# Retention followed by token mixing on one core: decay folded into q and v, head pairs on 128 partitions, and a hand-ordered pipeline of the two stages

## The chip, the cores and the metric

The kernel runs on one core of a Trainium2 chip. The metric is the device time of one launch in microseconds; in every run on record it is 1.65 to 1.84 us longer than the span of the same execution, which goes from the first to the last instruction. PE is TensorE (matrix products and transposes), PEld its weight loads, DVE is VectorE, ACT is ScalarE, POOL is GpSimd, and SP issues the transfers. A run counts as slow when it is over 1.5% above the fastest of its kernel; all times and ratios compared below are of fast executions, unless a median is called that of all runs.

## The reference

Eight heads of retention run over 768 tokens for each of four batches. The output, with the heads side by side, is the input of a mixing layer.

```python
gamma = 1.0 - 2.0 ** (-5.0 - np.arange(H))                 # H = 8, S = 768, D = 64, B = 4
for t in range(S):                                         # retention
    state = gamma * state + k_t (outer) v_t
    y[t] = scale * q_t @ state
x = y with heads joined                                    # B x 768 x 512
theta = x @ w_theta                                        # 512 x 512
zr, zi = x * cos(theta), x * sin(theta)
u = x + w_tok_r @ zr + w_tok_i @ zi                        # 768 x 768, over the tokens
out = u + relu(u @ w_ch)                                   # 512 x 512
```

Retention is computed in chunks of 128 tokens: products inside a chunk with a decay mask, and a state that carries the earlier chunks. There are 24 chunks and 24 mixing tiles of 128 tokens. A mixing tile needs all six chunks of its batch.

## The kernel before

All weights are loaded and transposed first. Then each batch runs the whole of retention and after it the whole of mixing.

```python
        for b in range(B):
            for c in range(nT):                       # retention, six chunks
                # ... load k, v, q of the chunk; one cast on ACT into kvq
                for src, dst, sc in ((kkc, kT, None), (qtmp, qTsc, qscale)):
                    tps = attPS.tile([D, H, P], BF, name="tps", bufs=2)
                    for h in range(H):                # 16 transposes, 64 wide
                        nc.tensor.transpose(tps[:, h, :],
                                            src[:, h * D : (h + 1) * D], ident)
                    # ... copy (k) or product with the decay (q) on DVE
                # ... kks = k times the decay, on POOL
                at_ps = attPS.tile([P, H, P], FT, name="at_ps", bufs=1)
                for h in range(H):                    # 8 score products, 64 deep
                    nc.tensor.matmul(at_ps[:, h, :], kT[:, h, :], qTsc[:, h, :], ...)
                nc.vector.tensor_mul(at, at_ps, Ddiag)
                # ... 8 value products, 8 state reads, 4 transposes of x, 8 state updates
            for t0 in range(nT):                      # theta, six tiles
                th_ps = moePS.tile([P, dm], FT, name="th_ps", tag="at_ps")
                # ... 4 matmuls; cos and sin on ACT; two products on DVE
            for t0 in range(nT):                      # token mixing, six tiles
                # ... 12 matmuls; u = y + x on DVE; 4 transposes of u; copy
            for t0 in range(nT):                      # channel mixing, six tiles
                # ... 4 matmuls; relu on ACT; sum on DVE; store
```

Of the kernel before, what the change touches and what calls it, by code (L numbers as in the profile page):

```python
# [19 lines left out]
PI = math.pi  # L20


def _bf16_view(ap: bass.AP) -> bass.AP:
    t = dataclasses.replace(ap.tensor, shape=list(ap.tensor.shape))
    ap2 = bass.AP(tensor=t, offset=ap.offset, ap=[list(p) for p in ap.ap])
    ap2 = ap2.bitcast(BF)
    new_pat = [list(p) for p in ap2.ap]
    new_pat[-1][0] *= 2
    new_pat[-1][1] //= 2
    return bass.AP(tensor=ap2.tensor, offset=ap2.offset + 1, ap=new_pat)  # L30


def _bcast_free(ap: bass.AP, n: int) -> bass.AP:
    return bass.AP(tensor=ap.tensor, offset=ap.offset,
                   ap=list(ap.ap) + [[0, n]])
# [3 lines left out]
def kernel(  # L39
# [10 lines left out]
):  # L50
    nc = tc.nc
# [5 lines left out]
    HD = dm  # L57
    HDp = HD + D
    scale = 1.0 / math.sqrt(D)
    gammas = [1.0 - 2.0 ** (-5.0 - h) for h in range(H)]  # L60

    qb = _bf16_view(q)
    kb = _bf16_view(k)
    vb = _bf16_view(v)


    const = ctx.enter_context(tc.tile_pool(name="const", bufs=1))

    ident = const.tile([P, P], BF)
    make_identity(nc, ident)  # L70
    identf = const.tile([P, P], FT)
    make_identity(nc, identf)

    iota_pp = const.tile([P, P], FT)
    nc.gpsimd.iota(iota_pp, pattern=[[0, P]], base=0, channel_multiplier=1,
                   allow_small_or_imprecise_dtypes=True)
    iota_f = const.tile([P, P], FT)
    nc.gpsimd.iota(iota_f, pattern=[[1, P]], base=0, channel_multiplier=0,
                   allow_small_or_imprecise_dtypes=True)
    colS_iota = const.tile([P, nT], FT)  # L80
    nc.gpsimd.iota(colS_iota, pattern=[[-P, nT]], base=127, channel_multiplier=-1,
                   allow_small_or_imprecise_dtypes=True)
    halfpi = const.tile([P, 1], FT)
    nc.gpsimd.memset(halfpi, PI / 2.0)
    lscale = const.tile([P, 1], FT)
    nc.gpsimd.memset(lscale, math.log(scale))
    zerob = const.tile([P, 1], FT)
    nc.gpsimd.memset(zerob, 0.0)

    Ddiag = const.tile([P, H, P], FT)  # L90
    qscale = const.tile([P, H, P], BF)
    colS = const.tile([P, nT, H], FT)
    gshift = const.tile([D, nT, H], FT)
    for h in range(H):
        g = gammas[h]
        lg = math.log(g)
        nc.scalar.activation(Ddiag[:, h, :], iota_pp, AF.Exp, bias=zerob, scale=-lg)
        nc.gpsimd.tensor_scalar(Ddiag[:, h, :], Ddiag[:, h, :], scalar1=1.0 / g,
                                scalar2=None, op0=ALU.mult)
        nc.gpsimd.affine_select(  # L100
            out=Ddiag[:, h, :], in_=Ddiag[:, h, :],
            compare_op=ALU.is_ge, fill=0.0, base=0,
            pattern=[[1, P]], channel_multiplier=-1,
        )
        nc.scalar.activation(qscale[:, h, :], iota_f, AF.Exp, bias=lscale, scale=lg)
        nc.gpsimd.tensor_scalar(qscale[:, h, :], qscale[:, h, :], scalar1=g,
                                scalar2=None, op0=ALU.mult)
        nc.scalar.activation(colS[:, :, h], colS_iota, AF.Exp, bias=zerob, scale=lg)
        for c in range(nT):
            nc.gpsimd.memset(gshift[:, c, h : h + 1], g ** (P * c))  # L110

    wconst = ctx.enter_context(tc.tile_pool(name="wconst", bufs=1))
    wth = wconst.tile([P, nD, dm], BF)
    wch = wconst.tile([P, nD, dm], BF)
    wtr = wconst.tile([P, nT, S], BF)
    wti = wconst.tile([P, nT, S], BF)

    with (
        tc.tile_pool(name="attA", bufs=2) as attA,
        tc.tile_pool(name="attB", bufs=2) as attB,  # L120
        tc.tile_pool(name="attPS", bufs=1, space=bass.MemoryType.PSUM) as attPS,
    ):
        for d0 in range(nD):
            for src, dst in ((moe_w_theta, wth), (moe_w_ch, wch)):
                tmp = attA.tile([P, dm], FT, name="wtmp")
                nc.sync.dma_start(out=tmp, in_=src[d0 * P : (d0 + 1) * P, :])
                nc.vector.tensor_copy(dst[:, d0, :], tmp)
        for src, dst in ((moe_w_tok_r, wtr), (moe_w_tok_i, wti)):
            for t0 in range(nT):
                tmp = attA.tile([P, S], FT, name="wtmpw")  # L130
                nc.sync.dma_start(out=tmp, in_=src[t0 * P : (t0 + 1) * P, :])
                wkrow = attA.tile([P, S], BF, name="wkrow")
                nc.vector.tensor_copy(wkrow, tmp)  # L133
                tp = attPS.tile([P, nT, P], BF, name="wtps", tag="tps", bufs=2)
                for s0 in range(nT):
                    nc.tensor.transpose(tp[:, s0, :],  # L136
                                        wkrow[:, s0 * P : (s0 + 1) * P], ident)
                nc.vector.tensor_copy(dst[:, :, t0 * P : (t0 + 1) * P], tp)
        for b in range(B):
            state_bf = attB.tile([D, H, D], BF, name="state_bf")  # L140
            st_ps = attPS.tile([D, H, D], FT, name="st_ps", bufs=1)
            x_sb = attB.tile([P, nT, dm], BF, name="x_sb")
            xT = attB.tile([P, nD, S], BF, name="xT")

            for c in range(nT):
                kvqin = attA.tile([P, 3 * HD], FT, name="kvqin")
                nc.sync.dma_start(
                    out=kvqin[:, :HD].rearrange("p (h d) -> p h d", h=H),
                    in_=k[b, :, c * P : (c + 1) * P, :].rearrange("h s d -> s h d"))
                nc.sync.dma_start(  # L150
                    out=kvqin[:, HD : 2 * HD].rearrange("p (h d) -> p h d", h=H),
                    in_=v[b, :, c * P : (c + 1) * P, :].rearrange("h s d -> s h d"))
                nc.sync.dma_start(
                    out=kvqin[:, 2 * HD :].rearrange("p (h d) -> p h d", h=H),
                    in_=q[b, :, c * P : (c + 1) * P, :].rearrange("h s d -> s h d"))
                kvq = attA.tile([P, 3 * HD + D], BF, name="kvq")
                nc.scalar.copy(kvq[:, : 3 * HD], kvqin)  # L157
                kkc = kvq[:, :HDp]
                vvc = kvq[:, HD : HD + HDp]
                qtmp = kvq[:, 2 * HD : 2 * HD + HDp]  # L160
                kT = attA.tile([D, H, P], BF, name="kT")
                qTsc = attA.tile([D, H, P], BF, name="qTsc")
                for src, dst, sc in ((kkc, kT, None), (qtmp, qTsc, qscale)):
                    tps = attPS.tile([D, H, P], BF, name="tps", bufs=2)
                    for h in range(H):
                        nc.tensor.transpose(tps[:, h, :],  # L166
                                            src[:, h * D : (h + 1) * D], ident)
                    if sc is None:
                        nc.vector.tensor_copy(dst, tps)
                    else:  # L170
                        nc.vector.tensor_mul(dst, tps, sc[:D])  # L171
                kks = attA.tile([P, HDp], BF, name="kks")
                nc.gpsimd.tensor_mul(  # L173
                    kks[:, :HD].rearrange("p (h d) -> p h d", h=H),
                    kkc[:, :HD].rearrange("p (h d) -> p h d", h=H),
                    _bcast_free(colS[:, c], D))

                at_ps = attPS.tile([P, H, P], FT, name="at_ps", bufs=1)
                for h in range(H):
                    nc.tensor.matmul(at_ps[:, h, :], kT[:, h, :], qTsc[:, h, :],  # L180
                                     start=(h % 4 == 0), stop=(h % 4 == 3),
                                     skip_group_check=True)
                at = attA.tile([P, H, P], BF, name="at")
                nc.vector.tensor_mul(at, at_ps, Ddiag)  # L184

                y_ps = attPS.tile([P, H, D], FT, name="y_ps", bufs=2)
                last = (c == 0)
                for h in range(H):
                    nc.tensor.matmul(y_ps[:, h, :], at[:, h, :],  # L189
# [10 lines left out]
                for d0 in range(nD):  # L200
                    nc.tensor.transpose(tpf[:, d0, :],
                                        x_sb[:, c, d0 * P : (d0 + 1) * P], ident)
# [88 lines left out]
```

## Time and profile before

| | before |
|---|---|
| time, median of 3 runs | 314.29 us |
| span of the profiled execution | 318.5 us |
| mean granted PE clock | 0.885 |
| PE busy | 235.5 us (74%), 1832 matmuls |
| DVE, ACT, POOL busy | 174.9, 86.2, 42.0 us |
| share of the chain that is not PE | 45% |

The lines are shown in the prediction below. In a strip, each digit is the busy share of a fortieth of the span in tenths. The chain starts at the last instruction and goes back, at each step to what released it. In a row of a stretch, each engine has its busy microseconds and in brackets its number of instructions; the granted clock and the DMA share follow.

The profiled execution of the kernel before would itself count as slow: a span of 318.5 us makes a time of some 320 us, where the fastest run took 313.55 us. The views of the profiled execution are read here for what waits for what, not to the per cent.

### The profile page before, as it was taken

The numbers are of one execution on the slowest core, as the hardware profiler recorded it, in microseconds if no ns is written. First come the engines' busy times: TensorE is split into PE (matmuls) and PEld (weight loads), VectorE is DVE, ScalarE is ACT, GpSimd is POOL, SyncE is SP. The second block draws the span as 40 slices with busy tenths as digits, with TensorE's granted clock in tenths as the row PEclk, the third lists the DMA queues.
The fourth block names the chain that finished last, engine by engine and source line by source line (L and its number), as shares of the span: only waits on it lengthen the run. The fifth ranks groups of instructions, "written<-read, shape, count | busy, mean of one in ns | idle before, by whom it ended". The sixth has DMA issues, their size and how long they took to land.

```text
span 318.5 us, 4555 instructions
## 1 busy us (share of the span) xinstructions
PE 235.5 (74%) x1832; PEld 140.0 (44%) x1832; DVE 174.9 (55%) x292; ACT 86.2 (27%) x122; POOL 42.0 (13%) x110
## 2 busy tenths in 40 slices
PE   0344677975699589886898578658985997778981
PEld 0222566842244368642343467323434785223430
DVE  2754557763444588843344899534347887233342
ACT  8000421236301231344102333441022330331022
POOL 8830221111000021210000022200000220000000
PEclk9999999979999975659999998799999657558999
DMA  6889975774000457763002298640013620000013
GB/s 225 271 258 254 195 151 112 149 141 99 1 2 12 155 126 160 151 125 66 2 0 94 107 197 184 117 99 0 2 66 132 145 55 3 0 0 1 2 66 132
DMA packets 81238, 32.28 MB, mean 101 GB/s; under 512 B 75585, under 2 KB 75585, under 8 KB 81217
## 3 DMA queue, kind: packets, MB, share of 16 engines
q1 hardware_dynamic: 81216, 31.99, 41.0%
q8 instruction: 14, 0.23, 0.3%
q14 instruction: 8, 0.06, 0.1%
HBM read 25.69 MB, written 6.29 MB: 100 GB/s over the span
## 4 chain that ended last, share of the span: by engine, by line
PE 55%; DVE 19%; DMA 12%; ACT 9%; issue 3%; SPq 0%; POOL 0%; ACTq 0%; DVEq 0%
PE moe_y L238 10%; PE moe_y L241 10%; PE th_ps L223 9%; PE tps L166 7%; DMA out_dram<-ot 5%; DVE at L184 5%; PE at_ps L180 4%; DMA wtmpw<-in_moe_w_tok_r_dram 4%; ACT cos_t L228 4%; PE y_ps L189 4%; DVE ot L259 3%; ACT kvq L157 3%; PE y_ps L195 3%; DVE zr L230 2%; PE tpf L247 2%
## 5 line engine op out<-in xcount | busy, mean ns | idle before, releaser
L238 PE MATMUL moe_y<-zr,wtr 128*128 128x512 bf16 x144 | 46.5, 398 | 18.0 <-DVE zr L230 18.0
L157 ACT CAST kvq<-kvqin 128x1536 bf16<-128x1536 f32 x24 | 35.3, 1472 | 90.0 <-PE y_ps L189 62.4
L173 POOL TENSOR_TENSOR kks<-kvq,colS 128x512 bf16<-128x512 bf16 x24 | 25.0, 1042 | 218.5 <-ACT kvq L157 218.5
L166 PE MATMUL tps<-ident,kvq 128*64 128x128 bf16 x384 | 40.9, 274 | 8.2 <-ACT ot L258 5.5
L166 PEld LDWEIGHTS <-kvq 128*64 128x64 bf16 x384 | 32.9, 144 | 13.8 <-issue 8.9
L258 ACT ACTIVATE ot<-o_ps 128x512 f32<-128x512 f32 x24 | 14.3, 597 | 84.9 <-PE o_ps L254 66.6
L241 PE MATMUL moe_y<-zi,wti 128*128 128x512 bf16 x144 | 35.6, 379 | 0.0
L223 PE MATMUL th_ps<-wth,xT 128*128 128x512 bf16 x96 | 33.3, 482 | 1.3 <-ACT sin_t L229 1.3
L184 DVE TENSOR_TENSOR at<-at_ps,Ddiag 128x1024 bf16<-128x1024 f32 x24 | 29.2, 1218 | 5.7 <-PE at_ps L180 5.1
L244 DVE TENSOR_TENSOR u<-moe_y,x_sb 128x512 bf16<-128x512 f32 x24 | 16.6, 691 | 26.8 <-PE moe_y L241 26.8
L230 DVE TENSOR_TENSOR zr<-x_sb,cos_t 128x512 bf16<-128x512 bf16 x24 | 10.8, 449 | 36.9 <-ACT cos_t L228 36.9
L228 ACT ACTIVATE cos_t<-th_ps,halfpi 128x512 bf16<-128x512 f32 x24 | 16.5, 688 | 52.4 <-PE th_ps L223 52.4
L254 PE MATMUL o_ps<-wch,uT 128*128 128x512 bf16 x96 | 23.3, 378 | 5.8 <-ACT ot L258 5.6
L136 PE MATMUL wtps<-ident,wkrow 128*128 128x128 bf16 x72 | 9.9, 309 | 22.1 <-DVE wkrow L133 22.1
L259 DVE TENSOR_TENSOR ot<-ot,u 128x512 f32<-128x512 f32 x24 | 16.5, 688 | 17.2 <-ACT ot L258 17.2
L223 PEld LDWEIGHTS <-xT 128*128 128x128 bf16 x96 | 10.4, 112 | 32.3 <-issue 27.0
L180 PE MATMUL at_ps<-qTsc,kT 64*128 64x128 bf16 x192 | 19.4, 259 | 5.5 <-DVE qTsc L171 5.4
L198 DVE CAST x_sb<-y_ps 128x512 bf16<-128x512 f32 x24 | 16.5, 689 | 12.3 <-PE y_ps L195 11.6
L241 PEld LDWEIGHTS <-wti 128*128 128x128 bf16 x144 | 13.9, 98 | 20.8 <-issue 5.2
L238 PEld LDWEIGHTS <-wtr 128*128 128x128 bf16 x144 | 14.1, 103 | 14.7 <-issue 3.4
L189 PE MATMUL y_ps<-kvq,at 128*128 128x64 bf16 x192 | 12.9, 225 | 9.6 <-DVE at L184 9.6
L180 PEld LDWEIGHTS <-kT 64*128 64x128 bf16 x192 | 15.7, 116 | 6.5 <-issue 4.3
(46 smaller groups left out, 237.8 us busy)
## 6 DMA issues: line engine op xcount, KB each, us to landing
kvqin<-in_k_dram SPq DMA_DIRECT2D x24, 256.0 KB, 3.2
kvqin<-in_v_dram SPq DMA_DIRECT2D x24, 256.0 KB, 4.1
kvqin<-in_q_dram SPq DMA_DIRECT2D x24, 256.0 KB, 4.3
out_dram<-ot SPq DMA_DIRECT2D x24, 256.0 KB, 2.0
wtmpw<-in_moe_w_tok_r_dram SPq DMA_DIRECT2D x6, 384.0 KB, 4.1
wtmpw<-in_moe_w_tok_i_dram SPq DMA_DIRECT2D x6, 384.0 KB, 3.5
wtmp<-in_moe_w_theta_dram SPq DMA_DIRECT2D x4, 256.0 KB, 4.0
wtmp<-in_moe_w_ch_dram SPq DMA_DIRECT2D x4, 256.0 KB, 3.8
```

The source lines that it names most:

```text
L157: nc.scalar.copy(kvq[:, : 3 * HD], kvqin)
L166: nc.tensor.transpose(tps[:, h, :], src[:, h * D : (h + 1) * D], ident)
L173: nc.gpsimd.tensor_mul(kks[:, :HD].rearrange("p (h d) -> p h d", h=H), kkc[:, :HD].rearrange("p (h d) -> p h d", h=H), _bcast_free(colS[:, ...
L180: nc.tensor.matmul(at_ps[:, h, :], kT[:, h, :], qTsc[:, h, :], start=(h % 4 == 0), stop=(h % 4 == 3), skip_group_check=True)
L184: nc.vector.tensor_mul(at, at_ps, Ddiag)
L189: nc.tensor.matmul(y_ps[:, h, :], at[:, h, :], vvc[:, h * D : (h + 1) * D], start=(h == 0), stop=(last and h == H - 1), skip_group_check=True)
L223: nc.tensor.matmul(th_ps, xT[:, d0, t0 * P : (t0 + 1) * P], wth[:, d0, :], start=(d0 == 0), stop=(d0 == nD - 1))
L228: nc.scalar.activation(cos_t, th_ps, AF.Sin, bias=halfpi, scale=1.0)
L238: nc.tensor.matmul(y_ps, wtr[:, s0, t0 * P : (t0 + 1) * P], zr[:, s0, :], start=(s0 == 0), stop=False)
L241: nc.tensor.matmul(y_ps, wti[:, s0, t0 * P : (t0 + 1) * P], zi[:, s0, :], start=False, stop=(s0 == nT - 1))
L254: nc.tensor.matmul(o_ps, uT[:, d0, t0 * P : (t0 + 1) * P], wch[:, d0, :], start=(d0 == 0), stop=(d0 == nD - 1))
L259: nc.vector.tensor_add(ot, ot, u[:, t0, :])
```

## The change

The intent has three parts.

- Arithmetic. The decay goes into q and v by position: q gets gamma to the power of the position, v its inverse. What stays of the mask is a 0/1 triangle, and the state needs no decay. Two heads share the 128 partitions, so k and q of a chunk take 8 transposes instead of 16, and the state is kept as four 128x128 blocks with two heads on the diagonal: 4 state reads and 4 updates instead of 8 and 8. The retention output is produced transposed, as theta's matmul needs it.
- Buffers. Theta, both mixing results and the retention output rotate through three accumulators; everything that PE transposes rotates through two.
- Order. Work is cut into slots written by hand. A slot may hold one chunk and one mixing tile. The steps of a chunk (T transposes, A scores, Y values and state, X theta, Z products with cos and sin) lie in consecutive slots, so that one slot holds steps of up to five chunks. Mixing of a batch starts while the next batch's chunks run. The weights of mixing are loaded behind the first six chunks and transposed in slots 5 to 8.

```diff
-    for b in range(B):
-        for c in range(nT): ...           # whole retention of a batch
-        for t0 in range(nT): ...          # then theta, token mixing, channel mixing
+    tau[n] = n if n < nT else n + 3       # slot of a chunk's first step
+    ready = tau[b * nT + nT - 1] + 4
+    mu[m] = max(ready, mu.get(m - 1, 0) + 1)          # slot of a mixing tile
+    for n in range(NCH):
+        for off, f in enumerate("TAYXZ"):
+            stage[f, tau[n] + off] = n
+    # ... loads and weight transposes of the slot
+        if g("T") is not None: att_T(g("T"))
+        if g("Z") is not None: att_Z(g("Z"))
+        if g("O") is not None: moe_U(g("O"))          # 4 transposes of u
+        if g("M") is not None: moe_M(g("M"), 0)       # 6 of the 12 matmuls
+        if g("A") is not None: att_A(g("A"))
+        if g("O") is not None: moe_O(g("O"))          # channel mixing
+        if g("M") is not None: moe_M(g("M"), 1)       # the other 6, then u on DVE
+        if g("Y") is not None: att_Y(g("Y"))
+        if g("X") is not None: att_X(g("X"))
...
-    for h in range(H):
-        nc.tensor.matmul(at_ps[:, h, :], kT[:, h, :], qTsc[:, h, :], ...)
+    for j in range(NP):
+        for par in range(2):                          # the two heads of a pair
+            rows = slice(par * D, (par + 1) * D)
+            nc.tensor.matmul(at_ps[:, par, j, :], kqT[rows, j, :], kqT[rows, NP + j, :], ...)
...
-    nc.vector.tensor_mul(at, at_ps, Ddiag)            # float32 decay mask
+    nc.vector.tensor_mul(at, at_ps, _bcast_mid(mask, H))     # bf16 0/1 mask
```

(The diff is cut to its core and put side by side; guards and argument lists are shortened.)

## The prediction

> **What bounds the kernel now.** I read the page's engine shares and strips first, then the chain that ended last, then the busy times by stretch, and last the groups of instructions for durations. The shares and the 40-slice strips:
>
> ```profile
> PE 235.5 (74%) x1832; PEld 140.0 (44%) x1832; DVE 174.9 (55%) x292; ACT 86.2 (27%) x122; POOL 42.0 (13%) x110
> PE   0344677975699589886898578658985997778981
> DVE  2754557763444588843344899534347887233342
> DMA  6889975774000457763002298640013620000013
> ```
>
> No engine is full. The DMA strip rises and falls four times: attention (retention) of a batch loads data, then its token mixing (moe) runs with DMA at 0 to 3 tenths. The four batches run these two stages one after the other. The chain (share of the span):
>
> ```profile
> PE 55%; DVE 19%; DMA 12%; ACT 9%; issue 3%; SPq 0%; POOL 0%; ACTq 0%; DVEq 0%
> ```
>
> So 45% of the end is set by something other than PE: PE hands over to DVE or ACT inside a stage and waits. Busy time by stretch shows the third thing (columns: span, busy per engine, granted clock, DMA share, GB/s):
>
> ```profile
> 33.00:45.00 12.00, 8.36 (x84) 7.23 (x84) 6.82 (x9) 3.12 (x3) 3.13 (x3) 1.00 0.96 206
> ...
> 120.00:125.00 5.00, 4.67 (x48) 3.75 (x48) 3.89 (x6) 1.47 (x1) 0.45 (x1) 0.50 0.73 162
> ...
> 278.00:283.00 5.00, 3.38 (x9) 0.97 (x8) 1.42 (x4) 2.35 (x4) 0.00 (x0) 0.50 0.00 0
> 293.00:298.00 5.00, 5.00 (x30) 2.27 (x29) 2.44 (x5) 0.00 (x0) 0.00 (x0) 1.00 0.01 3
> ```
>
> In attention (120 to 125) and in the theta stage (278 to 283) PE runs at half clock, in dense token mixing (293 to 298) at full clock. The chain of the last batch's theta stage and of the start, in order of time:
>
> ```profile
> 27.00 4.61 DMA kvqin<-in_q_dram
> 33.23 1.93 PE tps L166 x16
> 283.43 1.72 PE th_ps L223 x4
> ```
>
> Four 512-column matmuls in 1.72 us are 430 ns each, and 16 transposes in 1.93 us are about 115 ns each, so PE was also slow at 33 us, where the clock column says 1.00: I trust the spacing, not that column, before the first change of clock. Attention starts only at 31 us, because all weights are loaded and transposed ahead of it.
>
> [...] 430 ns cold; warm, six of them in 1.46 us with the first's latency of 0.38, so (1.46-0.38)/5 = 216 ns. [...] the trace has 1.04 us for a 512-column product on POOL. [...] 206 GB/s at a 0.96 share for the 256-byte runs of q, k, v against 271 GB/s in the best slice of the weight load.
>
> **The change part by part.** The durations come from these groups:
>
> ```profile
> L166 PE MATMUL tps<-ident,kvq 128*64 128x128 bf16 x384 | 40.9, 274 | 8.2 <-ACT ot L258 5.5
> L173 POOL TENSOR_TENSOR kks<-kvq,colS 128x512 bf16<-128x512 bf16 x24 | 25.0, 1042 | 218.5 <-ACT kvq L157 218.5
> L184 DVE TENSOR_TENSOR at<-at_ps,Ddiag 128x1024 bf16<-128x1024 f32 x24 | 29.2, 1218 | 5.7 <-PE at_ps L180 5.1
> L244 DVE TENSOR_TENSOR u<-moe_y,x_sb 128x512 bf16<-128x512 f32 x24 | 16.6, 691 | 26.8 <-PE moe_y L241 26.8
> L228 ACT ACTIVATE cos_t<-th_ps,halfpi 128x512 bf16<-128x512 f32 x24 | 16.5, 688 | 52.4 <-PE th_ps L223 52.4
> ```
>
> PE, 1832 matmuls to 1480 by counting the compiled kernel. Per chunk of 128 tokens: 16 half-width transposes become 8 pair-wide ones; the transposed output goes into theta directly, and its 4 transposes make x instead; 8 score products and 8 value products stay; 8 state products and 8 state updates become 4 and 4. Warm, I take 60 ns for a transpose or a 128-column product with its weight load (four in 0.40 us, the first's latency 0.22: 0.18/3) and 57 ns for a score product (eight in 0.60 us). One chunk: 20 times 60 (8+4 transposes, 4+4 state) = 1.20, 16 times 57 = 0.91, theta 4 times 216 = 0.86, sum 2.98 us. One tile of token mixing: 12+4 wide matmuls at 216 = 3.46, 4 transposes 0.24, sum 3.70 us. Together 6.7 us, by 24 = 160 us, plus 72 weight transposes.
>
> DVE per chunk and tile: copy of k and q transposed at 128x1024 bf16 0.68 (as the 64x1024 copy), masking 1.22, x 0.42, both products with cos and sin in one 0.7 (estimate from 0.42 and 0.45 for half that), u 0.69, output 0.69: 4.4 us. ACT: x transposed 0.6, two state copies 0.8 (estimate), cos and sin 1.28, u transposed 0.5: 3.2 us. POOL: two products at 1.04 [...]. All below 6.7, so in a slot that holds both a chunk and a tile PE is the bound, and since each step of a chunk reads what a slot before produced, I expect few waits, and the PE is dense enough to keep the full clock.
>
> Start, up to the slot of the first mixing tile (slot 9). In the order of the load queue: 6 chunks of 786 KB at 206 GB/s = 3.82 us each, 22.9; theta weights 3.9; token weights 2 by 8.7 and channel weights 3.9 at 271 GB/s; chunk 6, counted from 0 (which this slot's first transposes need, in PE's fixed order ahead of mixing) 3.8; 2 to land first: 54 us[...]. The same on PE, at half clock as all attention at the start of the kernel before: chunks become ready every 3.8 us from 8.5 us on, a full cold slot takes 5.6 us (twice 2.98 less overlap of weight loads), 72 weight transposes at 107 ns are 7.7 us: slots 2 to 8 end near 23, 30, 35, 43, 49, 55, 59. I take 60 us.
>
> From there by slot: 3.1, 4.65, 5.4, three at 6.7, then 4.1 and two attention-only ones at 3.2 (DVE's 3.0 and PE's 2.98 about equal), nine full ones 60.3, the drain 6.2, 5.7, 4.8, 4.2, five mixing-only ones. In those the transposes of u come first and wait for the 0.69 us addition just started, some 1.0 us: 4.7 each, 23.5. The last tile (transposes, copy, matmuls, addition, store of 2.0) 5.5. Sum 154 us. With 60 that is 214; I add 4 us for clock drops in the attention-only slots and for handovers: a span of 218. The median time of the kernel before is 314.29 at a span of 318.5, so 0.987 of it: **215 us**, 100 less. The gain comes from the overlapped start (mixing's weights arrive beside attention), the stage gaps (PE's 45% of foreign chain) and the clock; fewer matmuls themselves are worth only 352 times 57 = 20 us.
>
> **The rivals.**
> First, the clock stays low: 30% of PE's stream is still short products and transposes, and attention before sat at 0.50 although PE was 90% busy. For it: 120 to 125. Against: each full slot has 16+4 wide matmuls, 4.3 of 6.7 us, and dense mixing ran at 1.00. Cold for half of the mixed stretch would add some 40 us: 255.
> Second, POOL or the loads bind the start: POOL must cast 12 token rows and a 2048-column weight between chunk 5 and chunk 6 [...], the second half of the rows can load only after the first is cast, and the queue holds chunk 6 behind them. [...] For it: all in one queue and in order; against: nothing else of POOL's is urgent then.
> Third, buffers: the score buffer is single, and four kinds of result share three accumulators; the theta matmul reuses the one that u's addition has to empty about 1 us earlier. A wait of 0.5 us in 24 slots adds 12: 227.
> Fourth, the other way: pairs in the two halves of the array overlap, halving 16 products: 0.45 us off 18 chunks, 8 us: 207.
>
> **Range and chances.** The DMA total of before, 41% of 318 us = 130 us, and the PE total, 165 us, are floors that no arrangement crosses, so below 200 is unlikely. One of rivals two and three with some cold time gives 235. Range 202 to 235. Even the first rival leaves 255, 19% under before, so slower is nearly excluded: faster by over 2% 0.98, within 0.015, slower 0.005.
>
> **What would show it.** PE busy near 90% and clock near 1.0 between 65 and 190 us; 216 ns wide matmuls with about 6.7 us per slot there; the first mixing matmul at 57 to 63 us; gaps of about 1 us before the transposes of u only in the last six tiles; the chain mostly PE with DMA at the start. I am wrong in the start if the first mixing matmul is beyond 66 us, in the clock if theta's four take over 1.3 us after 80 us, in the buffers if theta waits for u's addition, and in the pairing if eight score products take well under 0.6 us.

The kernel before casts nothing on POOL, so the durations put there for casts were not shown; with them POOL's share of a chunk and tile came to 2.7 us, the loads' side of the start to 54 + 2.7 = 57 us, and the second rival to 225 us. The total does not contain these terms: 60 us for the start were taken from PE's side. The sentence that begins with 430 ns speaks of 512-column matmuls; "cold" and "warm" stand for the spacings that the trace of before shows, 427 to 430 and 215 to 216 ns between such matmuls, 107 ns between weight transposes when cold. That PE in a full slot is dense enough to keep the clock rests on the row from 293 to 298 us alone (PE busy for 5.00 of 5 us at 1.00); what share of busy time keeps it was not shown. The 2 us to land, the 0.8 us for two state copies, the 0.5 us for u transposed on ACT and the 5.6 us of a cold slot were estimates. On the page of before, a store of 256 KB lands after 2.0 us, and ACT takes 0.39 us for 128 columns and 0.60 us for 512.

## More of the kernel before

In every run the time is 1.65 to 1.84 us longer than the span of the same execution.

`th_ps` has the tag of `at_ps`, of which there is one buffer: theta of a tile has to wait until both activations have read that of the tile before.

## The result

The changed kernel takes 203.32 us (median of 4 runs, 203.13 to 203.53), the kernel before on the same chip 314.11 us (4 runs, 313.55 to 322.85, one slow run among them). The ratio is 0.646, with a 95% interval of 0.642 to 0.649. A ratio here is the mean time of one kernel's fast runs over that of the other's of the same rounds, so it is not quite the ratio of the medians quoted beside it. The time lies in the predicted range, 12 us under the predicted 215.

The profile after, in the order in which the prediction read that of before. First the engine shares, the strips of PE, of the granted clock and of the transfers, and the chain that ended last:

```profile
PE 168.5 (83%) x1456; PEld 94.9 (47%) x1480; DVE 108.7 (54%) x153; ACT 79.0 (39%) x147; POOL 78.9 (39%) x105
...
PE   0235786898999999799999999999999999877872
...
PEclk9999998799999999999999999999999999999999
...
GB/s 143 245 284 218 221 356 394 400 203 233 220 175 229 221 213 255 253 258 260 231 228 235 61 52 55 52 28 27 52 55 52 28 25 55 52 62 83 64 52 52
...
PE 70%; SPq 10%; ACT 5%; DVE 5%; DMA 3%; issue 3%; POOL 2%; ACTq 0%; POOLq 0%
```

The four waves of the strip of before are gone: PE is at 9 for most of the run, and the clock is full after the first fifth (its record is at 1.00 from 37.4 to 201.2 us). PE's share of the chain rose from 55% to 70%, and most of the rest lies in the start, where the chain goes along the loads. (24 of the 1480 matmul records are missing in this trace.) The row of a stretch in the middle, in the columns of the prediction:

```profile
120.00:140.00 20.00, 19.84 (x180) 10.99 (x183) 13.82 (x20) 8.24 (x16) 6.27 (x7) 1.00 0.11 41
```

PE is busy for 19.84 of 20 us at full clock. The rate of a slot is read from the chain in order of time (start, duration, what), at the same place in three slots:

```profile
125.23 1.24 PE y_ps L248 x5
...
131.55 1.24 PE y_ps L248 x5
...
138.10 1.24 PE y_ps L248 x5
```

(One of the six matmul records of each group is missing.) The slots take 6.32 us here (the first chunk of a batch, which reads no state) and 6.55 us. The prediction had 6.7 us. The chain at the start:

```profile
22.07 6.46 DMA qf<-in_q_dram
28.67 1.04 POOL qb L145
...
49.44 2.60 PE y_ps L248 x12
```

The sixth chunk is there at 28.5 us, and the first mixing matmul starts at 49.3 us. The prediction had 57 to 63 us for it. At the end, in the slots with a mixing tile alone:

```profile
181.27 0.70 DVE u L253
181.97 0.05 issue
182.02 0.40 PE u_ps L259 x4
```

PE stands still while DVE computes u (0.70 us), because the transposes of u are its next instruction. Such a tile takes 4.64 us (transposes of u at 177.38 and 182.02 us). The group whose cost the folded decay and the bf16 mask might have lowered:

```profile
L173 DVE TENSOR_TENSOR at<-at_ps,mask 128x1024 bf16<-128x1024 f32 x24 | 29.3, 1221 | 6.4 <-PE at_ps L169 6.4
```

The masking takes 1221 ns; with the float32 decay mask it took 1218 ns.

### The profile page after: what moved, and what is told of

The parts are those of the page before. It is cut to its first block, busy times and chain, and to the rows that moved or that the text cites. A ratio compares the mean times of both kernels' runs of the same rounds, so it can differ in the third digit from the quotient of the medians.

```text
span 201.8 us, 3699 instructions
## 1 busy us (share of the span) xinstructions
PE 168.5 (83%) x1456; PEld 94.9 (47%) x1480; DVE 108.7 (54%) x153; ACT 79.0 (39%) x147; POOL 78.9 (39%) x105
## 4 chain that ended last, share of the span: by engine, by line
PE 70%; SPq 10%; ACT 5%; DVE 5%; DMA 3%; issue 3%; POOL 2%; ACTq 0%; POOLq 0%
PE y_ps L248 29%; PE o_ps L268 11%; SPq L77 10%; PE th_ps L226 9%; PE yT_ps L192 4%; PE kq_ps L156 3%; DMA qf<-in_q_dram 3%; PE at_ps L169 3%; PE u_ps L259 3%; DVE u L253 3%; PE st_ps L200 3%; PE x_ps L223 3%; PE yT_ps L186 2%; ACT cs L231 2%; ACT cs L230 1%
## 5 line engine op out<-in xcount | busy, mean ns | idle before, releaser
L248 PE MATMUL y_ps<-z,wti 128*128 128x512 bf16 x144 | 54.6, 379 | 0.9
L248 PE MATMUL y_ps<-z,wtr 128*128 128x512 bf16 x127 | 48.1, 379 | 0.0
L159 DVE COPY kqT<-kq_ps 128x1024 bf16<-128x1024 bf16 x24 | 16.6, 690 | 30.1 <-PE kq_ps L156 30.1
L173 DVE TENSOR_TENSOR at<-at_ps,mask 128x1024 bf16<-128x1024 f32 x24 | 29.3, 1221 | 6.4 <-PE at_ps L169 6.4
L147 POOL TENSOR_TENSOR vb<-vf,vsc 128x512 bf16<-128x512 f32 x24 | 26.4, 1099 | 13.9 <-PE st_ps L200 7.8
L145 POOL TENSOR_TENSOR qb<-qf,qsc 128x512 bf16<-128x512 f32 x24 | 25.0, 1043 | 12.6 <-DMA qf<-in_q_dram 12.6
L271 DVE SCALAR_TENSOR_TENSOR ot<-o_ps,u 128x512 f32<-128x512 f32 x24 | 16.5, 685 | 18.6 <-PE o_ps L268 18.2
L236 DVE TENSOR_TENSOR z<-cs,x_sb 128x1024 bf16<-128x1024 bf16 x24 | 18.7, 781 | 8.8 <-ACT cs L231 8.7
L253 DVE TENSOR_TENSOR u<-y_ps,x_sb 128x512 bf16<-128x512 f32 x24 | 16.6, 692 | 11.3 <-PE y_ps L248 11.2
L230 ACT ACTIVATE cs<-th_ps,halfpi 128x512 bf16<-128x512 f32 x24 | 16.5, 687 | 10.5 <-PE th_ps L226 10.4
```

Of the source, the lines that this page charges most:

```text
L145: nc.gpsimd.tensor_mul(qb.rearrange(r3, h=H), raw[n, "qf"], _bcast_last(qsc[:, c], D))
L147: nc.gpsimd.tensor_mul(vb.rearrange(r3, h=H), raw[n, "vf"], _bcast_last(vsc[:, c], D))
L173: nc.vector.tensor_mul(at.rearrange("p a j t -> p (a j) t"), at_ps.rearrange("p a j t -> p (a j) t"), _bcast_mid(mask, H))
L230: nc.scalar.activation(cs[:, 0, :], th_ps, AF.Sin, bias=halfpi, scale=1.0)
L236: nc.vector.tensor_mul(zs[b][:, c], st[n]["cs"], _bcast_mid(xs[b][:, c, :], 2))
L248: nc.tensor.matmul(y_ps, wT[r][:, s0, t0 * P:(t0 + 1) * P], zs[b][:, s0, r, :], start=(s0 == 0 and r == 0), stop=(s0 == nT - 1 and r == 1))
```

## The experiments

The theory after the result: the hand order makes the difference, since it fills PE's waits inside a chunk with other chunks (the offsets of T to Z) and with mixing tiles (interleaving), and a PE that is filled also keeps its clock. Rival one: the arithmetic (pairs, folding) does most of it. Rival two: the clock is a cause of its own, lost wherever retention runs alone. For what is left of the time, the theory was that the start is bound by loads and that the waits for u cost a few microseconds.

Each kernel was timed in 3 to 5 rounds beside the kernel before on the same chip, whose median there was between 314.1 and 320.3 us. Medians of all runs are given, and the ratio to the kernel before. All results were correct, except that of e6. Its output is wrong, which doesn't matter for the time.

### e1_sequential: no interleaving

The offsets stay, but the chunks of a batch start when the mixing of the batch before ends.

```diff
-        tau[n] = n if n < nT else n + 3
+        tau[n] = (n // nT) * 15 + n % nT
-        if slot > 2 and slot + 5 < NCH:
-            load_chunk(slot + 5)
+        if g("T") is not None and slot > 2 and g("T") + 5 < NCH:
+            load_chunk(g("T") + 5)
```

> The changed kernel with its instructions kept, but a batch's retention starts only when the mixing of the batch before has had its last tile, so no slot holds both. Theory (the interleaving saves mainly the hand-over idle time that one stage cannot hide by itself): per batch 9 retention slots of at most 2.9 us, about 18 us, plus 6 mixing slots at the 4.64 us that the last tiles of the changed kernel take, 28 us, so 46 us a batch after the first, and about 220 us in all, the clock staying near 1.0. Rival (the interleaving's main gain is the clock: retention alone lets it drop to half as in the kernel before): retention slots of some 5 us, granted clock near 0.5 in them, 250 us or more. Second rival (the order matters little, the folded arithmetic and the buffers are the gain): below 208 us.

Measured: 227.36 us, ratio 0.722 (0.716 to 0.727), clock 0.99. Interleaving is worth 24 us. The strip of the clock, and the instructions of DVE for z in a stretch with retention alone (from the time line; the masking of one slot between them):

```profile
PEclk9999997999999999999999999999999999999999
```

```profile
85.44 1.29 DVE L236 TENSOR_TENSOR z<-cs,x_sb 128x1024 bf16<-128x1024 bf16 x1 [0.16 <-ACT cs L231]
86.65 1.21 DVE L173 TENSOR_TENSOR at<-at_ps,mask 128x1024 bf16<-128x1024 f32 x1
...
88.72 1.03 DVE L236 TENSOR_TENSOR z<-cs,x_sb 128x1024 bf16<-128x1024 bf16 x1
...
91.74 1.03 DVE L236 TENSOR_TENSOR z<-cs,x_sb 128x1024 bf16<-128x1024 bf16 x1 [0.53 <-ACT cs L231]
```

The clock stays full with retention alone (1.00 in each of the stretches from 80 to 98, 126 to 145 and 173 to 192 us), so rival two has no ground here. Products z start 3.0 to 3.3 us apart, so a slot with a chunk alone takes about 3 us; the prediction had 3.2. The nine slots from 74.25 to 96.49 us take 22.2 us together, where 18 were expected.

Much of the 24 us is not retention's. The waits of PE for u in this run, and below in the changed kernel:

```profile
PE u_ps L259 <- DVE u L253: 17.5, 24, 0.8
...
PE u_ps L259 <- DVE u L253: 5.4, 8, 0.8
```

Here every one of the 24 mixing tiles makes PE wait for u, 17.5 us in all; in the changed kernel 8 do, 5.4 us. That is some 12 of the 24 us, and e7 below takes this wait away by order alone. What interleaving is worth on top of e7's order was not run; half as much is an estimate from these waits.

### e2_unpaired: products of one half after the other

```diff
-        for j in range(NP):
-            for par in range(2):
+        for par in range(2):
+            for j in range(NP):
                 rows = slice(par * D, (par + 1) * D)
```

> The changed kernel with the eight score products in the order of all low-half heads, then all high-half heads, instead of alternating. Theory (two products in the two halves of the array run beside each other, which is why eight take 0.33 us from first start to the next group's start instead of the 0.45 us that I predicted): each group of eight grows to 0.45 to 0.55 us, 24 groups add 3 to 5 us where PE is the bound, 206 to 208 us. Rival (the short spacing comes from the warm clock and weight loads alone, not from alternating halves): spacing unchanged, 203 us.

Measured: 203.19 us, ratio 0.645. Nothing changed, and the expectation missed. The start times of the eight score products of one chunk, in nanoseconds from the trace (not a view of the page):

```
after, issued pair by pair:     120089 120093   120155 120159   120211 120214   120267 120270
e2, four of rows 0-63, then
    four of rows 64-127:        119694 119707   119760 119773   119816 119829   119871 119885
```

In both kernels eight products start as four pairs, 3 to 4 ns apart in the changed kernel and 13 ns in e2, with some 56 ns from pair to pair. In the compiled program of e2 the four products of the lower rows do stand before the four of the upper rows. In e9, where all eight use the same rows, they take 0.62 us, the last of them some 0.23 us, so they start within some 0.39 us (an estimate from these two), here within 0.19 us. So the reading is that PE runs the two halves beside each other, also when the program lists one half after the other. The trace does not name the half of a product; this part is inference. As a way to undo the pairing, the run failed.

### e3_flat: no offsets

All steps of a chunk but Z lie in one slot. The chunks of later batches start three slots later, so that retention keeps its lead over mixing.

```diff
-        tau[n] = n if n < nT else n + 3
+        tau[n] = n if n < nT else n + 6
-        ready = tau[b * nT + nT - 1] + 4
+        ready = max(tau[b * nT + nT - 1] + 1, 9)
-        for off, f in enumerate("TAYXZ"):
+        for off, f in zip((0, 0, 0, 0, 1), "TAYXZ"):
# and loads by slot + 2 instead of slot + 5
```

> The changed kernel with the four PE steps of one chunk in one slot (only the product with cos and sin a slot later) instead of one step per slot for four chunks; slots of mixing kept. Theory (the staging by slots hides the copies between the steps): in a slot with mixing the copies of k and q and the masking still lie beside mixing matmuls, but the copy of the retention output (0.59 us on ACT) opens a PE gap of about 0.7 us per slot, and in retention-only slots three gaps of 0.7 to 1.4 us: 215 to 225 us. Rival (the order within a slot suffices, depth is not needed): below 207 us.

Measured: 233.56 us, ratio 0.740 (0.732 to 0.748), clock 0.961. The chain in two full slots:

```profile
126.43 0.59 ACT xT L206
...
127.07 0.40 PE x_ps L223 x4
...
133.50 0.59 ACT xT L206
```

The offsets are worth 30 us, more than the 12 to 22 expected. PE now waits in each slot for ACT's copy of the retention output that it has just produced, and a slot takes 7.07 us. The first mixing matmul comes at 62.3 us, 13 us later than in the changed kernel. From there to the end it takes 18 us more. About half of that, 9.2 us, lies in the three slots without token mixing (95.7 to 115.2 us: 19.5 us, in the changed kernel 10.3 us); the rest is in the slots that hold both, most of them 7.07 us where the changed kernel has 6.54.

### e4_before_theta2: two theta accumulators in the kernel before

```diff
-                th_ps = moePS.tile([P, dm], FT, name="th_ps", tag="at_ps")
+                th_ps = moePS.tile([P, dm], FT, name="th_ps", tag="y_ps", bufs=2)
```

> The kernel before with one edit: the theta accumulator takes turns over two buffers (those of the retention output and of the mixing sum) instead of one. Theory (part of the old time is theta waiting for ACT to empty its only accumulator, 2.5 us a tile warm and 3.5 us cold, which the change removes with three accumulators): a tile falls to 1.3 to 2 us, 24 tiles save 15 to 30 us, 285 to 300 us. Rival (half-clock matmuls and the other hand-overs set that stage anyway): above 308 us.

Measured: 298.14 us, ratio 0.944 (0.931 to 0.956). From the waits of this run (engine and line, released by, total us, times, longest):

```profile
ACT cos_t L228 <- PE th_ps L223: 26.5, 9, 9.3
```

ACT waited 52.4 us in all for theta before (the last of the groups in the prediction) and 26.5 us now. Beside the kernel before on the same chip, the single buffer cost some 17 us of the old time (5.6%, with an interval from 4.4 to 6.9%). That could have been had with one line; no slots are needed for it.

### e5_weights_first: no loading of weights beside retention

```diff
-    load_chunk(0)
-    load_chunk(1)
     load_w512("th", moe_w_theta)
-    for n in range(2, 6):
-        load_chunk(n)
# ... all weights loaded, cast and transposed ahead of slot 0, then chunks 0 to 7 loaded
```

> The changed kernel with all weights loaded, cast and transposed ahead of the first chunk, as the kernel before does; the rest kept. Theory (the loads bind the start, and what must have landed before the first mixing matmul is the same in either order, 12.4 MB; only the drain of the retention pipeline after the last of them is exposed): first mixing matmul about 3 to 6 us later than 49.3 us, 206 to 210 us. Rival (the overlap of weight work with retention is itself worth the 10 us and more of casts, transposes and PE work of the six chunks): first mixing matmul beyond 58 us, 213 us or more.

Measured: 209.99 us, ratio 0.664 (0.662 to 0.667). The first mixing matmul is at 55.1 us, 5.8 us later, and the kernel is 6.7 us longer. Overlapping the weights with retention is worth only that much here.

### e6_long_runs: chunks loaded as one long run (wrong result on purpose)

```diff
-                out=t, in_=src[b, :, c * P:(c + 1) * P, :].rearrange("h s d -> s h d"))
+                out=t, in_=src[b].rearrange("h s d -> (h s d)")[c * P * dm:(c + 1) * P * dm]
+                .rearrange("(p h d) -> p h d", p=P, h=H))
```

It moves as many bytes in 2 KB runs instead of 256-byte ones, and other elements than are needed.

> Wrong result on purpose: q, k and v are read in the same bytes per load, but as contiguous 2 KB per partition instead of eight runs of 256 bytes, so the numbers land in the wrong places; all instructions and shapes kept. Theory (the start is bound by loads, and the 256-byte runs make the chunk loads slow, some 240 GB/s against 360 to 400 for the weights): seven chunks of 786 KB take about 2.1 instead of 3.2 us each, first mixing matmul at 41 to 44 us, 195 to 199 us. Rival (POOL, 14.7 of 20 us busy from 20 to 40 us, or PE's chain binds the start): at 47 us or later, above 201 us.

Measured: 195.56 us, ratio 0.618 (0.615 to 0.621). The first mixing matmul is at 42.8 us, 6.5 us earlier. Between 20 and 50 us the transfers ran at 385 to 397 GB/s; the changed kernel loads chunks at 218 to 221 GB/s where nothing else loads (15 to 25 us). So the start does depend on the loads, as e5 says from the other side, and 8 us hang on the short runs. It is no version to use, only a measure.

### e7_late_u: transposes of u half a tile later

```diff
-        if g("O") is not None:
-            moe_U(g("O"))
         if g("M") is not None:
             moe_M(g("M"), 0)
+        if g("O") is not None:
+            moe_U(g("O"))
         if g("A") is not None:
             att_A(g("A"))
-        if g("O") is not None:
-            moe_O(g("O"))
         if g("M") is not None:
             moe_M(g("M"), 1)
+        if g("O") is not None:
+            moe_O(g("O"))
```

> The changed kernel with two groups moved in PE's order: the transposes of u after the first half of the next tile's mixing matmuls instead of before, the channel matmuls after the second half. Theory (in the last tiles PE waits about 0.9 us a tile for the addition u, because its transposes come first): five mixing-only tiles fall from 4.64 to about 3.75 us, and a few gaps at slots 10 and 15 go, 197 to 200 us. Rival (the gap comes back elsewhere, at the channel matmuls or in a full slot at the accumulators): 202 us or more.

Measured: **194.76 us** (194.5 to 196.46), ratio 0.617 (0.613 to 0.621). This is the fastest of all, and correct. The gain of 8.6 us is above the 3 to 6 expected. The chain of two mixing tiles at the end, and a stretch in the middle:

```profile
170.27 0.22 PE u_ps L259 x4
170.50 1.29 PE y_ps L248 x6
...
173.95 0.22 PE u_ps L259 x4
```

```profile
140.00:160.00 20.00, 20.00 (x178) 11.25 (x176) 11.86 (x18) 9.78 (x19) 0.00 (x0) 1.00 0.11 40
```

A tile takes 3.68 us instead of 4.64 us, with DVE's u and ACT's copy of it hidden behind six matmuls each. The same wait had also been in the first mixing slots, where the chain of the changed kernel contains DVE's u at 52.1 and 57.1 us and that of e7 does not, and in the slots where retention runs out. That is why more than the last six tiles gained.

### e8_rows: token weights by pairs of row blocks

A mixing tile needs only its own row block of both token weights. Here the blocks are loaded and transposed in pairs, one pair per slot from slot 8 on, instead of all ahead of the first mixing tile; the transposes of u stay early.

```diff
-        if 5 <= slot < 9:
-            for i in range((slot - 5) * 3, (slot - 4) * 3):
-                w_tok(i // nT, i % nT)
+        if 8 <= slot < 14:
+            for r in range(2):
+                w_tok(r, slot - 8)
# and the loads in that order, with chunks 6 and 7 between; the channel weight is cast in slot 9, not 7
```

> The changed kernel with the token weights loaded by pairs of the two matrices' row blocks, each pair worked in the slot before the mixing tile that needs it, instead of all twelve before the first tile; chunk 6 loads after two pairs. Theory (a mixing tile needs only its own row block of both, so the first mixing matmul has to wait for 8.1 instead of 12.4 MB; it then is bound by retention's drain at about 40 us): first mixing matmul at 39 to 43 us, all 6 to 9 us earlier, 194 to 198 us. Rival (the work moved into the mixing slots costs PE, ACT or POOL there what is gained, or chunks 7 and on come late): above 200 us.

Measured: 214.32 us, ratio 0.678 (0.675 to 0.681): slower, a miss. Pieces of the chain:

```profile
28.71 8.21 DMA kf<-in_k_dram
...
38.33 7.42 DMA kf<-in_k_dram
```

And what SP's list waited for between 20 and 62 us:

```profile
SPq L91 <- POOL wrow L276: 4.7, 2, 4.4
```

The first mixing matmul did come 3 us earlier, at 46.3 us. But chunks 6 and 7 now land behind rows and the channel weight, 8.2 and 7.4 us after their issue, and then SP's list stands for 4.4 us, because the six row buffers are emptied by POOL in the new, later order; the next chunk's load is behind the row that waits. Retention then comes late, and PE with it.

### e9_no_pairs: one head per transpose, k, q and state on 64 partitions

```diff
-        kq_ps = psum.tile([P, 2 * NP, P], BF, name="kq_ps", tag="tr", bufs=2)
-        for i, src in enumerate((s["kb"], s["qb"])):
-            for j in range(NP):
-                nc.tensor.transpose(kq_ps[:, i * NP + j, :], src[:, j * P:(j + 1) * P], ident)
+        for nm in ("k", "q"):
+            t_ps = psum.tile([D, H, P], BF, name=nm + "_ps", tag="tr", bufs=2)
+            for h in range(H):
+                nc.tensor.transpose(t_ps[:, h, :], s[nm + "b"][:, h * D:(h + 1) * D], ident)
# ... scores from rows 0 to 63 alone; 8 state reads and 8 updates of 64x64
```

> The changed kernel with the head pairs undone in all that needs them: k and q go through 16 half-width transposes and two copies to 64 partitions, the score products all use rows 0 to 63, the state keeps 64 partitions with 8 products and 8 updates per chunk and one copy; folding, staging and order kept. Reordering the eight score products in e2 did not undo the pairing (eight starts in four close pairs in both), this does. Theory (pairing saves PE and DVE work that lies on the path while PE is the bound): per chunk 8 more transposes at 60 ns, 0.2 us for the scores and as much for the state products, one DVE copy of 0.68 us more and a wait of the transposes of u for it; 0.8 to 1.2 us in the 18 chunks beside mixing, 216 to 226 us. Rival (the order hides it, PE has slack that the profile does not show): below 210 us.

Measured: 226.70 us, ratio 0.720 (0.715 to 0.725). The count is back at 1832 matmuls, and PE is busy for 194.0 us. The eight score products here, all on the same rows, from the time line:

```profile
121.02 0.62 PE L165 MATMUL at_ps<-qT,kT 64*128 64x128 bf16 x8
```

They take 0.62 us; in the changed kernel the group takes 0.40 us. Pairs are worth 23 us, of which a part is a side effect: k, q and u now take turns in two transpose buffers, and DVE's copy of k is on 4% of the chain.

### e10_flat_sequential: neither offsets nor interleaving

The edits of e1 and e3 together: the arithmetic, the buffers and the overlapped weight load stay, both orders go.

```diff
+        tau[n] = n if n < nT else (n // nT) * 12 + n % nT + 3
+        ready = max(tau[b * nT + nT - 1] + 1, 9)
+        for off, f in zip((0, 0, 0, 0, 1), "TAYXZ"):
```

> The changed kernel with both orders undone: the four PE steps of a chunk in one slot, and no mixing beside retention; what stays is the folded arithmetic, the pairs, the transposed output, the loads and buffers. Theory (the two parts of the order add up, 24 us from e1 and 30 us from e3, and a chunk alone is a chain of hand-overs of about 5.5 us with nothing to fill it, so that more than the sum is lost and the clock falls): 260 to 285 us, granted clock below 0.95. Rival (each alone already loses what the other would hide, so the two overlap): 235 to 255 us.

Measured: 296.84 us, ratio 0.942 (0.935 to 0.949), even longer than expected; a chunk alone, put at 5.5 us there by estimate, takes 7.18 us (scores at 161.89 and at 169.07 us). Shares, and the chain as it passes from one chunk (cs, z) to the masking of the next:

```profile
PE 207.2 (70%) x1480; PEld 110.1 (37%) x1480; DVE 112.4 (38%) x153; ACT 81.2 (27%) x147; POOL 81.6 (28%) x105
...
PEclk9997779799999777769999777759999777779999
```

```profile
160.69 0.69 ACT cs L230
161.38 0.59 ACT cs L231
...
161.99 0.84 DVE z L236
162.83 1.15 DVE at L173
```

Undoing both costs 94 us, while each alone costs 24 and 30 us. The spans add up exactly: PE is busy 38.7 us longer than in the changed kernel (207.2 less 168.5) with the same matmuls, and idle 55.6 us longer (88.9 less 33.3), together 94.3 us (24 missing records in the changed kernel's trace make its busy time a microsecond or so too small). Most of the first part is the clock: in each of the four retention stretches its record falls (to 7 tenths in the strip, to 0.72 in the mean from 164 to 170 us, where theta's four matmuls take 1.91 us, against 1.03 us at 159.6 us), and theta's matmuls alone keep PE busy for 38.4 us, 21.3 us in the changed kernel. The latency of the first matmul after each wait is in it too: PE has 108 idle gaps, in the changed kernel 52, and there one transpose of u takes 219 ns from start to end, where transposes in a row start 56 ns apart. So the clock is lost when the two orders are undone together, and hardly when one of them is kept: 0.99 in e1, 0.961 in e3, 0.871 here, and 0.885 in the kernel before.

What keeps the clock is not shown. Here it fell to 0.72 on average (164 to 170 us) where PE's longest idle time in that chunk and the one before was 1.40 us and PE was busy for 4.64 of 6 us; in the kernel before it was at 0.50 with PE busy for 4.67 of 5 us; in e1, retention with PE busy for 16.4 of 19 us (126 to 145 us) kept 1.00. PE's longest gap was 0.33 us in that stretch of the kernel before, and 1.18 us in that of e1 (to 141 us). So neither the longest gap nor the busy share tells these three apart, and no run separates the causes.

### e11_rows_late_u and e12_rows_again: a better start on top of e7

e11 puts e7 and the row pairs of e8 together, with twelve row buffers instead of six, so that no row waits for a buffer.

```diff
-        t = io.tile([P, S], FT, name="wtok", bufs=6)
+        t = io.tile([P, S], FT, name="wtok", bufs=12)
# and the edits of e7 and e8, with chunk 6 loaded after the first pair, chunk 7 after the second
```

> The late transposes of u (e7) together with the token weights by pairs of row blocks (e8), mended: 12 load buffers for the rows instead of 6, so that no load waits for a cast in the one load queue, and chunk 6 right after the first pair. Theory (e8 lost because its later loads stood in the queue behind rows that waited for POOL to free a buffer, landing chunk 6 8 us and chunk 7 7 us after their issue): first mixing matmul at 38 to 43 us, 184 to 190 us. Rival (the loads are simply too slow for a row pair and a chunk per slot, 1.57 MB in 6.5 us, or POOL is): at best equal to e7, 193 us or more.

Measured: 197.62 us, ratio 0.628 (0.625 to 0.630), 2.9 us longer than e7. The first mixing matmul is at 44.5 us, 4.6 us ahead of e7, but PE is busy for only 18.3 of the 20 us from 60 to 80, where in e7 it is busy for all 20. In four slots the first transposes wait for the copies of the row pair just before them (0.58, 0.55, 0.31 and 1.38 us), and the first half of the first tile ran at half clock (427 ns between its matmuls, to 47.1 us).

e12 casts the rows a slot earlier, transposes them behind the mixing matmuls, and starts the later chunks two slots later.

```diff
+        if 7 <= slot < 13:
+            for r in range(2):
+                w_cast(r, slot - 7)
+        if 8 <= slot < 14:
+            for r in range(2):
+                w_tok(r, slot - 8)            # behind the second half of M
-        tau[n] = n if n < nT else n + 3
+        tau[n] = n if n < nT else n + 5
```

> e11 mended once more. In e11 the first mixing matmul came at 44.5 us because POOL's cast of the channel weights stood ahead of the second row pair and waited 3.5 us for its load, and the slots after it were 0.9 us longer because the first transposes of a slot waited for the copies of the row pair just before them. Here the casts of a pair come one slot earlier, its transposes after the mixing matmuls, the channel cast after the second pair, and the chunks of the second batch start two slots later so that the first mixing slots need no new chunk. Theory: first mixing matmul at 39 to 42 us, 3 to 4 us of weight transposes moved into the mixing stretch, 188 to 192 us. Rival (from 40 us on rows and chunks together ask of the loads what they give, about 250 GB/s, so PE waits for chunks instead and nothing is gained over e7): 194 us or more.

Measured: 200.38 us, ratio 0.639 (0.636 to 0.641). The first mixing matmul came at about 41 us, as hoped, and the time won was given back. From the time line (start, duration, engine, line, what, and in brackets the idle time before it and its releaser):

```profile
74.13 0.75 SPq L272 DMA_DIRECT2D out_dram<-ot  x1
...
78.21 0.69 DVE L271 SCALAR_TENSOR_TENSOR ot<-o_ps,u 128x512 f32<-128x512 f32 x1 [5.88 <-DMA out_dram<-ot]
...
79.29 0.58 PE L259 MATMUL u_ps<-ident,u 128*128 128x128 bf16 x4 [4.40 <-DVE x_sb L228]
```

The first output tile was ready at 49.9 us, but its store was issued only at 74.1 us: in SP's one list it stands behind the loads of the chunks to come, which are issued one after another at the pace of the transfers, about 1.1 us each. The four output buffers were full by 67 us; DVE waited 5.88 us for the first store to land, and PE 4.40 us for DVE. The same wait of DVE is 0.4 us in the changed kernel, although there, too, the first tile is ready at 56.7 us and its store is issued only at 75.4 us. Rows in pairs start mixing earlier and thereby fill the output buffers earlier. Whether stores from another engine's list would keep the start won by e12 was not run; it stays open.

## Why the prediction was right, and where it was off

The predicted time was 215 us and the measured one 203.3 us; the range held it. In spans the miss is larger, 218 against 201.8 us. The step from span to time (0.987 of it) took the ratio of a median to the span of what would count as a slow execution; time is 1.7 us longer than span, so 218 should have become some 219.7. This error hid 4.5 us of the other, by luck. By its own steps:

- **The stretch from the first mixing slot.** Predicted 154 us plus 4. Measured from the transposes that open that slot (48.8 us) to the end of the span (201.8 us): 153.0 us. Its parts, predicted against measured: slots 9 to 17, 43.8 against 44.1 us; the nine full slots, 60.3 against 57.4 us; the drain, 20.9 against 22.4 us; five slots of mixing alone, 23.5 against 23.2 us; the last, 5.5 against 5.9 us. So the account of PE as the bound held in each part, the full slots 3 us too dear (pairs, below) and the drain 1.5 us too cheap, and the 4 us added for clock drops and handovers did not come.
- **The start.** This is the term that was mis-sized: 60 us predicted, 48.8 us measured. The first half was right: six chunks and the theta weights landed at 28.5 us, against 22.9 + 3.9 + 2 = 28.8. After that, the token and channel weights arrived at 356 to 400 GB/s where I took 271. And "at half clock as all attention at the start of the kernel before" failed: PE had its full clock from about 27 us on, but for 34 to 37 us (in the record, 1.00 from 27.2 us and 0.50 from 34.0 to 37.4 us). Twelve weight transposes took 0.83 us, less the first's latency of 0.22 some 55 ns each, where I took 107 ns. Runs e5 and e6 show by +6.7 and -7.8 us that loads set a part of the start.
- **The three slots without token mixing.** Predicted 4.1, 3.2 and 3.2 us; measured 4.85, 2.64 and 2.85 us (transposes of k at 82.60, 87.45, 90.09 and 92.94 us). The first is longer because PE waits there for ACT's copy of u (1.06 us). "Clock drops in the attention-only slots" did not occur: the clock is 1.00 there.
- **The gaps before the transposes of u.** Their size was right (4.64 us a tile against 4.7). "Only in the last six tiles" was wrong: PE waits for u 8 times in the changed kernel, and e7 shows what that costs.
- **The rivals.** The first, a clock that stays low, did not come (0.99 in the mean), and e10 shows a case in which the clock falls (0.871). The second did not bind: POOL's casts took 0.91 us a row and 1.90 us for the channel weight, 12.8 us in all. The third, theta waiting for u's addition, does not appear among the waits. The fourth came true, as no run had shown before this one: with both halves of the array in use the score products take less time than with one. From the first of eight score products to the next group it is 0.33 us, in e9 with one half alone 0.55 us. The saving of 0.22 us a group is the half that the rival had named. Against the assumed 0.46 us only 0.13 us shows, since the estimate had left out the change between whole and half array: the first score product starts 0.31 us after the wide matmul before it, where wide ones follow each other by 0.216, and the next group 0.15 us after the last pair, where pairs follow by 0.056, in e9 as well. With the value products (0.35 us) that is some 0.24 us a chunk, 4 us in 18 chunks, where I had put 8.
- **Where the gain comes from.** The prediction named the overlapped start, the stage gaps and the clock, with 20 us for fewer matmuls. Pairs measured 23 us (e9). The overlapped weights measured only 6.7 us (e5). The gaps and the clock together are the 94 us of e10, out of 111; 12 of them are again waits for u (24 in e10, 17.5 us). These parts overlap and do not add up: undoing offsets alone costs 30, interleaving alone 24. Rival one of the experiments, that the arithmetic does most of it, falls with e10: with all of the arithmetic in place and the order undone, 5.8% of the old time is gained. Folding the decay did not shorten the masking (1218 to 1221 ns); it is part of what POOL now does more (42.0 to 78.9 us, with casts among it). No run undid the folding alone.

## What to carry to other kernels

When the chain hands over between engines inside one unit of work, offset the steps of several units before anything else, and put the dense stage beside the one that waits: here only the loss of both brought the half clock back in every batch (0.871 in the mean, against 0.99 and 0.961 when one was lost). Then look for the one instruction in a hand-written order that asks for a result just started; moving the transposes of u by six matmuls gave 8.6 us in 203, more than any correct change to the start did, and half of what interleaving seemed to give was this same wait. Before advancing loads in a single list, ask what stands behind them: in two of three attempts (e8, e12) a load or a store stuck there ate what the earlier start had won.
